# A hand-written order of 2,756 steps and its list of masked tiles, written anew

## The chip, the cores and the metric

One core of a Trainium2 chip runs the whole program. The metric is device time in microseconds (us) of one execution: median 465.35 us of three runs before the change (464.76 to 468.1). The engines are named as in the profile: PE is TensorE (PEld its weight loads), DVE VectorE, ACT ScalarE, POOL GpSimd, SP SyncE, which here only starts transfers.

## What is computed

Attention over 8 batches x 8 heads, 576 rows of 64, where only scores within tau = 0.02 of the row's maximum count; then a feed-forward layer with the largest of three products as its activation. Cut to the core:

```python
scores = (q @ k.transpose(0, 1, 3, 2)) / sqrt(64)
thresh = max(scores, axis=-1, keepdims=True) - tau
scores = where(scores >= thresh, scores, -1e9)
attn = exp(scores - max(scores)); attn = attn / (sum(attn) + 1e-9)
x = (attn @ v).transpose(0, 2, 1, 3).reshape(4608, 512)
h = maximum(maximum(x @ w1, x @ w2), x @ w3)     # 768 wide
out = h @ w_out                                   # 4608 x 512
```

## The kernel before

**Stages.** Four heads of a batch form a quad, so there are 16 quads, two to a batch. The 576 rows of a head are cut into chunks of 128; the rests of the heads share a chunk, so a quad has 9 chunks and the program 144. Each chunk has two tiles of scores (r = 0, 1), each 128 rows by 576 keys: 288 tiles. For every tile TensorE makes the scores in float32 (S). A quad's q and k must be turned first (T), by TensorE in float32, copied out by ScalarE (q) and VectorE (k); GpSimd copies a half-swapped q. Then, tile by tile, VectorE finds the row maximum (m), ScalarE makes exponents (e), and a last pass gives numerators and row sums. VectorE takes reciprocals (r), GpSimd scales to bf16 (p, once per tile), and SyncE starts one transposing DMA per chunk (t), which puts the chunk into ptq. When all nine chunks of a quad are there, TensorE makes the product with v (O, two per quad), which VectorE and ScalarE copy to xt. Per batch then follow 18 hidden pieces (F, and B for the second half of the same piece, evacuated by h and v) and the outputs (F and B, evacuated by u, stored by o). The last batch is split in two parts.

**The mask list.** A tile has two ways. If its digit in MASKED (line 24) is 1, VectorE copies the scores negated while it takes the maximum, ScalarE makes plain exponents, and VectorE sets those below exp(-tau) to zero and sums (k, a VectorE step). If it is 0, ScalarE makes two passes, the second with the sum (n). So a 1 moves work of some 0.7 us from ScalarE to VectorE.

**The order.** Every step of every engine stands in one string, ORDER (lines 38 to 70), read from left to right (lines 659 to 666). The class in lines 80 to 97 ties each instruction to the one before it on its engine, so each engine carries out its own letters in exactly the written order; between engines only data and buffers make them wait. S, T, O and F carry a digit, the PSUM bank pair (0 to 3) that the piece is written to. A piece can start only when the bank's last owner has been read. The other letters: a and c copy turned q and k out of PSUM, q is the swapped copy, l the next load of a quad (in turn: last columns of q and of k, 64 KB each, then the main parts of q and of k, 512 KB each, then v in two pieces of 256 KB and two of 32 KB), y a cast of v, g a load of 512 KB of weights and z its cast on GpSimd, x and w the copies of a product, h, v, u those of F pieces, o a store. The letters l, g, t and o all go to SyncE's one queue.

What each letter does is in issue (lines 596 to 657). The buffers: two of each loaded q, k, v and of ptq, four chunks of z, six of P.

Of the kernel before, what the change touches and what calls it, by code (L numbers as in the profile page):

```python
# [43 lines left out]
BmS3ezremF2pghkS1zetBmnF0vS3epgBnmF2pS1vetBmT0hS3rcpeF1S2rmpBmpteF0vpeBknS3ztF1nmS2vyeT3gzBmlO0hrlpalnpF1wle
T3ytBcnS0kS2nlmzO3nlrmeqlvelS2pS0rwxrmyF1npmS3gqBekqeF2vntpBmnS0pS1hmpgeS2mpeS3rmpeF0tmpeBrnS1pvS2tepmF0nzS3
metBrmpT2nS1vpaS3tnS0zmS2ermtpF1nkpnmS3eByrtmepkepF2lemlukS0utkBermnpoT1rekpoS0ecO3lupmtnpO1weoqurktpnS3T0xr
wS2mapoF1meT3qlS0cetBqmF3phS2kleqBmlF1nyF0lrnvBelpBrvS3yhpS2mnF1ptmS0epBmeF2ptvnF3BkeS1tvBnS0mhF2rmepS3rBepm
S1nytvF0peS3mpBnlmS2yetvT3eF1maS0lkBeqlS3mhlF2rmeplT1nlcpS0eBlrmpF1tnS3kpeBmnlO0qvernvtpT2S3wapS1nrmF2ptnS0m
# [5 lines left out]
rmBeptmeykS1yelS2mupS3lumO1temekT0oeF2ronwplakT3nT1qcS0nBpmnqtraS3peO1mqukuqonT0wS3rocpxS2lmeF0ptrF1mepBkpS3
thBremS0plvF2eptS3mS1ymeBlmF0pelS3veBmF2thS1keBknF0lmF3nlBveBlrknF2plS1rhvBnpmF3nS0pvtBepmF2rS1vtepBmpF0hT3k
tBerS2pavS1npF3mS0qmteBrmepO2vnpeS1twnS3mS0nF2meS1meBrmF0phS3knpBemO2eqvterkpT1xT0wS3caF2pnmT1qBtnrcF0pnvS3q
lBempF1lhS2rkyleBtmF0pvS3epBlrnmS1ypnvF2pterS3mpuS0meS2ptF1meymetS3knS0keBomnrmS2eplS3umpF0luroemptS2ekpT1em
T3oBakteqcT1nS2klaS3rmulpO1umoqeorkyeS0S2npmO3nprtwepmS1xpT0wtnmF2qS3ecpBlermF0qlhkS1pteBmnF2S3pvleBymlnF1vS
0eBtnmF2hS3keBlrmpF1nlvF0pnBlrpS2etvBynmS3S1hlrpmF2erpS0mteBpmeS3pvtnF0S1myeyF2pmeBktBeF3khT1vBaS2vnT0qS1rmp
O3meqcepS2wnF0tS1rnmpT3nmBpS2arvpS1temF3qeO0mpeketT2kxBnwS1clF0hrlmS2pnlBrkyeF3lmF1BrveqlBkpnF0lS2vhlBprmT3t  # L60
S1pvaS2pmeF0tS3mpeBkpteF1vnS2pmulS0moS1eF3metrmepS2knpS1S0nmBertmpekpS1nF2mertmpeS0kepS1mBuuqmtnS0keO3omeoku
O1urkoperowT2xpwT0cS3aqtS1nmF2qrF0myepBekS3yBhmF1pnS2vqteBmpnT0F3rcpelS2vBpnlS0mtphS1meS3mteF2knBmleS0lrnvpS
1ermF2plnS3pmteBpmF1eS0rveptBmnpF2kS3htBemF1nS0rvpleBmpF2nlrS3vpelT0mBtpaS1khS3qtmS0eqO2nmekerS3mpS1nmpO0ewt
ermpF2xwT3kpeF0cnBF1ntvT3BnkBarvS2phT3rrF0mqS1pceBmqtT3nS2pvS1ampS0eF3mpteF2mqeBkByeT1vhS0cT3pS2amF1qtnmF3qe
BkqBevS0nrF2vpT1rmupS3noS2cpnS0mpF1etmyeyrmpS2etkBepmnS3ktuS0urmF2peompnorS1kpeS3tmeS0BpmemteS1kuS0urS3kopnO
2ormepeO1pmnpweO0twrxmO2pxkS1eptS0xmnF3mS2teBkF0hmF1nBkS3ervF2peBmpBveS0ytF3hmS1F2emBkF0eBrvnpBrF1vphS3kpBtF
2mF0pveBytS3nyvO1kO2xrmF1xpBrkepS2BhmF3nptF0vepBF1ntvBS2hBmF3vS0eBrmpF1F2vpeBnS3thS0mBmF1eS3veBmnF0vO2urkepo
# [632 lines left out]
```

## Time and profile before

| what | value |
|---|---|
| median of three runs | 465.35 us |
| span of the profiled execution | 465.6 us |
| first piece of the order on TensorE, end of its last | 7.7 us, 460.8 us |
| POOL: P from z | 288 times 0.81 us, waits for DVE rs 58.5 us in all |
| ACT: e and n of tiles without mask | 0.74 and 0.68 us, 179 each |
| DVE: maximum of a tile | 0.75 us, 288 in all |
| transposing DMAs on SP | 144, 3.9 us from issue to landing (median) |
| main q and k loads, 512 KB each | 15 and 15, 4.4 and 5.5 us |
| bytes moved | 87.44 MB, 188 GB/s mean |

Times in the profile are those of one execution. An engine's idle time matters only where that engine, or one that it holds up, sets the end. The profile names for each idle stretch the instruction that ended it; a wait for a transfer is shown as DMA and the tile that it fills. The granted clock is the share of its full clock that TensorE was given.

### The profile page before, as it was taken

How to read it: one execution, taken by the hardware profiler on the slowest of the kernel's cores; microseconds unless marked ns; L12 is line 12 of the kernel's file. 1: busy time of each engine (PE TensorE's matmuls, PEld its weight loads, DVE VectorE, ACT ScalarE, POOL GpSimd, SP SyncE). 2: the span in 40 equal slices, each digit the busy share in tenths (PEclk: the TensorE clock that was granted, in tenths of full speed). 3: DMA queues.
4: the chain of work that ended last, by engine and by line, in shares of the span. 5: the costliest groups of instructions: out<-in, count | busy, mean ns of one | idle time of the engine just before them, and what ended most of it. 6: DMA issues, size and time to landing. Idle time of an engine off the chain costs nothing.

```text
span 465.6 us, 14101 instructions
## 1 busy us (share of the span) xinstructions
PE 437.9 (94%) x5188; PEld 314.1 (67%) x5188; DVE 403.9 (87%) x1115; ACT 394.0 (85%) x794; POOL 318.7 (68%) x416
## 2 busy tenths in 40 slices
PE   7778788999999999979999999999999999999995
...
PEclk8995899999999999979999999999999999999999
...
GB/s 256 242 210 232 199 222 246 166 237 275 216 232 183 212 161 230 221 215 135 207 214 229 130 189 212 212 196 220 160 190 224 153 84 223 105 102 66 173 32 103
DMA packets 212773, 87.44 MB, mean 188 GB/s; under 512 B 185824, under 2 KB 199648, under 8 KB 212704
## 3 DMA queue, kind: packets, MB, share of 16 engines
...
q14 instruction: 28, 0.23, 0.1%
...
## 4 chain that ended last, share of the span: by engine, by line
PE 70%; DVE 11%; ACT 11%; issue 5%; DMA 2%; POOL 0%; SPq 0%; ACTq 0%; DVEq 0%; POOLq 0%
PE sc L89 25%; PE ph L89 25%; ACT z L89 9%; PE po L89 8%; PE o L89 8%; DVE z L89 6%; PE tp L89 3%; DVE unused L89 2%; DMA ptq<-P 1%; DMA qm<-in_q_dram 1%; DVE kt L89 1%; DVE hT L89 1%; ACT xt L89 1%; ACT hm L89 1%; DVE hm L89 1%
## 5 line engine op out<-in xcount | busy, mean ns | idle before, releaser
L89 POOL TENSOR_SCALAR P<-z,rs 128x576 bf16<-128x576 f32 x288 | 229.5, 810 | 94.7 <-DVE rs L89 58.5
L89 PE MATMUL sc<-kt,qt 64*128 64x320 f32 (+2 forms) x640 | 192.7, 442 | 4.2 <-ACT z L89 2.2
L89 PE MATMUL sc<-kt,qs 64*128 64x256 f32 (+2 forms) x640 | 189.7, 431 | 6.2 <-ACT z L89 4.1
L89 PE MATMUL ph<-xt,w 64*128 64x288 bf16 (+2 forms) x2160 | 170.9, 283 | 1.2 <-DVE xt L89 0.3
L89 PEld LDWEIGHTS <-w 64*128 64x128 bf16 (+1 forms) x2160 | 125.0, 94 | 41.1 <-issue 12.6
L89 ACT ACTIVATE z<-sc,nm 128x576 f32<-128x576 f32 x179 | 129.9, 739 | 21.1 <-DVE unused L89 15.5
L89 DVE TENSOR_SCALAR_CACHE_REDUCE unused<-sc 128x576 bf16<-128x576 f32 x179 | 132.2, 749 | 8.2 <-PE sc L89 7.0
L89 ACT ACTIVATE z<-z 128x576 f32<-128x576 f32 x179 | 121.3, 680 | 0.3
L89 PEld LDWEIGHTS sc<-kt,qs 64*128 64x128 f32 (+1 forms) x640 | 93.2, 182 | 27.3 <-ACT z L89 7.4
L89 PEld LDWEIGHTS sc<-kt,qt 64*128 64x128 f32 (+1 forms) x640 | 93.1, 182 | 18.2 <-ACT z L89 6.7
L89 DVE SCALAR_TENSOR_TENSOR z<-z 128x576 f32<-128x576 f32 x109 | 93.3, 861 | 1.0 <-ACT z L89 0.9
L89 DVE TENSOR_SCALAR_CACHE_REDUCE z<-sc 128x576 f32<-128x576 f32 x109 | 81.1, 750 | 11.7 <-PE sc L89 9.9
L89 ACT ACTIVATE z<-z,nm 128x576 f32<-128x576 f32 x109 | 82.0, 771 | 9.8 <-DVE z L89 9.7
...
L89 PE MATMUL po<-wo,hT 64*128 64x512 bf16 (+1 forms) x480 | 54.2, 356 | 0.1
L89 ACT ACTIVATE hm<-ph 128x576 bf16<-128x576 f32 (+2 forms) x54 | 32.1, 595 | 16.2 <-PE ph L89 15.9
L89 DVE TENSOR_TENSOR hm<-ph,hm 128x576 bf16<-128x576 f32 (+2 forms) x54 | 36.9, 684 | 9.9 <-PE ph L89 9.1
L89 PE MATMUL o<-ptq,vb 128*64 128x64 bf16 (+2 forms) x544 | 40.6, 288 | 3.4 <-DMA ptq<-P 3.1
L89 PEld LDWEIGHTS <-hT 64*128 64x128 bf16 (+1 forms) x480 | 30.2, 97 | 17.6 <-issue 3.9
L89 DVE TENSOR_TENSOR hT<-ph,hm 128x576 bf16<-128x576 f32 (+2 forms) x54 | 37.0, 685 | 2.9 <-PE ph L89 1.4
L89 PEld LDWEIGHTS <-vb 128*64 128x64 bf16 x544 | 22.9, 113 | 20.9 <-issue 8.5
L89 ACT ACTIVATION_READ_ACCUMULATOR z<-z 128x1 f32 x179 | 35.4, 198 | 0.0
...
## 6 DMA issues: line engine op xcount, KB each, us to landing
...
ptq<-P SPq DMA_TRANSPOSE x144, 3.9
...
```

The lines of the kernel that those rows point to most:

```text
L89: ins = fn(*a, **kw)
```

## The change

Both strings are replaced. MASKED has 109 ones as before, at other places. ORDER has the same letters in the same numbers; their sequence and the bank digits differ. The first eight tokens now begin with a weight load and five loads of the second quad, where three of those loads came before the first S. No other line differs. Cut to the head, the stretch up to the first product of batch 3 (the O2 in the last of the three lines, on either side), and the end:

```diff
 MASKED = """
-101001010100010100100100100001010100000101000011000101010100000100100100
-000000111101010100001000101000001100100011011000110011000010100010010001
-000100110011000100111000010000101001001100011110000100100010010000111010
-100100101111001001000001000110110001100001010111001110011100100001101100
+101000100110000110011100001010010001100010001000101000010000100000100010
+000011110101100001001001001001000001011100101011000110001010010000010011
+001010011101100000101100100001001010000110011111000001000100000110000101
+001001001101100000110001000100101000001100010011100101110110000001111111
 """
...
 ORDER = """
-lllS0lmyS1eyS2lmlS3kelmnS0lmegS1repmgS2kyemnS3pT0meS1tmeymaS3S2knS0llremplekT3pnlrS1meqmnpmteprceT2qketS3pS0
-anT1rmS2lpnmS3qlempntrcS2pekT1eptS0mnqmelprkalS3petS1mnS2qrmnS0lperlmpetkpeT3mnlS1pmetS2mpnremptekyS0nS2qmlT
...
-lS0kuS3lakS1onF2rmpemlepS0rkepBtmnpmF3erqktepT1uBuconqroS0yuS2pumoS1pT3mteS0ympeO2koayntmO3ewqelrkS1qxlT2wS0
-rnmlpF3mlepcS1BleyF0tmphS2kpeBlmF3nF1lyveBtrknBpS0vhS2lpnrmF3S1pmetBpmeS0veS1tF2mnS3meBlmnF1F0lveBrelkpS2lBh
-mF3npF1vBetkS0nrrBvpF2mhpS3BeptmS1nyvT0T3nrmO2parcyetpS0ewqS3mnO1pmeptkeS2qT3xwS0mayF1meqF3kBeqBrnvT2pS0hclS
...
-O1S0xpS3mF1tmekS0eBmweF3rkpnkuS2pnBorrmupteF0pF1hF2nopvF0tuvpF1rhF2pvF0tvF1phF2vF0tvF1hF2uvF0ovF3hoF1vF2vF0h
-F3vF1vO2uoO0wF3xF1F2hF0vF1vF2hF0vF1vF2hF0vF1vF2hF0vF1vF2hF0vF1vF2hF0vBvF1uuooBF2uuouoo
+glllllS0lylS1mylyeS2zmlkS3lelmnlT0mS1aS2rmeqS0meqmeS3pnkT1pT0nrcaptemS0yeS1mgS2eympeS3mqtnT1S0mqnS2knrceprmS
+1epkepeS3mnyS0rkptemnS2pmnlzmS3erremtpT0empS1eklpaS2kgnS0ptnmeprrmlS1epS3mleS2pmlS0eplmetpmeS1knS3tkernkS2pt
...
+mparrcpS2uS1pumtS0empS3emqoS1eF2mqlemqleS3kplnS0mBlepmlekT1teO3kunktO0urcpnrrwlS2nplS1wxmpS3lmpS0eompS1eF2mt
+peF3meBkBetS0khF1nrmF2pnBvpBerrvS3phS0mtnpS1mF2peS3mtpeBmeF1yvF0etByknBvnS2tS3rhmpS1melpS0meF3lmF2elBkeBlvT1
+ntF0nvT3BacS2ohS1rrmlpnF3lmF0peoBkpeBovnT2oS1qavS3tnprO2rmpmleqS0wtnT3pS1mepO2mteqkeqF0nS1cxBywmpnS3rS2hytmS
...
+1tmBeBkO2vO0rvpF3kpF1uketeF3kekBwrrkpBukxpuF2F0hptF1vF2pvF0hF1tvF2rvpF0hF1vpF2vF0thF1uvF2uvF0hoF3vF1vF2hoF0v
+oO3oO1wovF2xF3uoF0F1hF2vF0vF1hF2vF0vF1hF2vF0vF1hF2vF0vF1hF2vF0vF1hF2vBvF0uuooBF1uuouoo
 """
```

More of the change, by code (lines that the diff above doesn't have):

```diff
@@ L44 @@
[L44 to L48, printed above, removed]
@@ L49 @@
-qBempF3hS1kqteO2meykT0rxrBwpceS2yvnS0ylmF1nlS3pmelF2pmtBeBkpeS0vhlS3nrtmF1pS2mepBrlmeF3ptS0vepS2mnBtmF1evnT2
-lS0kuS3lakS1onF2rmpemlepS0rkepBtmnpmF3erqktepT1uBuconqroS0yuS2pumoS1pT3mteS0ympeO2koayntmO3ewqelrkS1qxlT2wS0
-rnmlpF3mlepcS1BleyF0tmphS2kpeBlmF3nF1lyveBtrknBpS0vhS2lpnrmF3S1pmetBpmeS0veS1tF2mnS3meBlmnF1F0lveBrelkpS2lBh
-mF3npF1vBetkS0nrrBvpF2mhpS3BeptmS1nyvT0T3nrmO2parcyetpS0ewqS3mnO1pmeptkeS2qT3xwS0mayF1meqF3kBeqBrnvT2pS0hclS
-1ynmtF3nS2mpBelmpF1elS0vetBmnF3rS2veplBmnpF1S0rhkptBemF3nprS2vleBpmS0tnpvF1emS3tuS2rkepS1nrF0mopnmepS3tmeS2p
@@ L54 @@
[L54 to L67, printed above, removed]
-O1S0xpS3mF1tmekS0eBmweF3rkpnkuS2pnBorrmupteF0pF1hF2nopvF0tuvpF1rhF2pvF0tvF1phF2vF0tvF1hF2uvF0ovF3hoF1vF2vF0h
@@ L69 @@
-F3vF1vO2uoO0wF3xF1F2hF0vF1vF2hF0vF1vF2hF0vF1vF2hF0vF1vF2hF0vF1vF2hF0vBvF1uuooBF2uuouoo
+glllllS0lylS1mylyeS2zmlkS3lelmnlT0mS1aS2rmeqS0meqmeS3pnkT1pT0nrcaptemS0yeS1mgS2eympeS3mqtnT1S0mqnS2knrceprmS
+1epkepeS3mnyS0rkptemnS2pmnlzmS3erremtpT0empS1eklpaS2kgnS0ptnmeprrmlS1epS3mleS2pmlS0eplmetpmeS1knS3tkernkS2pt
+nmnprmtepmS1eqS0melpmT2ntrmT3pnrcpatekS3pekS2eqnrS1mtnqmS0pemepS3tmeqS2kepT1lnrcnprtmS0nT1pmS3epmgS2atpmeO1k
+yermeO0knptrerT3wpnT2wcS1aptmnS3pS2xmptS1emzS0emeS3zgmeS2lrmpnS0lmO1eplmeplknO3qlnrwleplwkS1xqgS2ertmF3npF0m
@@ new lines @@
+eT1pBrteBkyhS2cpnS3mpS1nvF2npmF0eqBmeqBrrvepS3tkhT2pS1nmS0lapmetS2pmeS3mzeF0mF1ezgBrnF2vpgnBktByeF0rvhpS3ntS
+2pmF1npmBeBqrveT3zncT0F2taqvS3nBpmnS0tprhS1rmpeS3mtpS2emeyS0mteF1zmeF3kBelqBnvgF2pngT0vBnqlrS1cphS3lrmnS0plm
+O2eplmeptS1ewpS3nmF0znmS2lBezkgO3etymyS1vegkF0ntF2wnrrmpBxBpveS3phS0mtnF1prmeBprS2evptS3nmF0pnS1mplBermS3ztn
+S2vnzS1meS0tmpeF3mperkS2petBmepmS0tkuF1ukelkT3elBkntrarmpS2uS3pmulS0eymtO1empnrO2kpewS3xpwS1elmpF2lmF0eyqBrl
+keT3ytBhcF1pnT2vT3qlaBclnS0qvlS2nqtF3mnyF1meS0pBemBthrrF2kpeS3vnBpmF0nS1pveBrprS3mhtS2pmeS0pmeS1tpmF2emF3peB
@@ new lines @@
+tkeT0BvaF1onvqT2T0tBcqaS3nkqS0lhrmS2nlpmF1elpF3meBlkBelF0vntS2rvnBpS1mhplS3melF0mS2teBrmepS1rkpO3emnqO2tnrvp
+nwyS0xlprwS3emoF2pmoT1eyBpctS3evyF0nS1mtnS2pmBeympF1hkS3eyF2rekT0ptBamBnpS0veF3qtvS1urmnpS2mF3epketT0nkT1Bnr
+mparrcpS2uS1pumtS0empS3emqoS1eF2mqlemqleS3kplnS0mBlepmlekT1teO3kunktO0urcpnrrwlS2nplS1wxmpS3lmpS0eompS1eF2mt
+peF3meBkBetS0khF1nrmF2pnBvpBerrvS3phS0mtnpS1mF2peS3mtpeBmeF1yvF0etByknBvnS2tS3rhmpS1melpS0meF3lmF2elBkeBlvT1
+ntF0nvT3BacS2ohS1rrmlpnF3lmF0peoBkpeBovnT2oS1qavS3tnprO2rmpmleqS0wtnT3pS1mepO2mteqkeqF0nS1cxBywmpnS3rS2hytmS
@@ new lines @@
+1emF0peF3mpeBrkBpetF2vnF1pBnvS0thkS3nmF2BmeBveF0rrvpT1uS3kapS0nmS2F1pmtepmeS3rktepS0mnS2pmlBelrmeplS3kupS0lu
+rmS2elpF1mnoqmeS0qreS2lmpS3elmBpelmptekO0nketO2ukurrnwpT3T1xwpcS0aF2ymyT3tpS1ceBqmS3thqF0meF2pknBtBnvF1nS3rt
+rvpeBmS0phS2lmepS1lmyS3etF0meyF2mpeBkBetF1knF3vnBBrvhpS0nvT1pF2nmF3takBeS0rvplBmS1phlrS2remplF3mpleF0klBpeS1
+lvnS2lpmnBtrO3mepvnptS2nwS1emF0mF3eBrkepS2hBrmS1nptvS0npT2meO3qmeycqlT0xT1wyS2lacF3ntmyT0yeF1kqBatrBrevqF0hk
+S2pnoS3mF1pmBteBpveS2qntS0vpnF3mprS1mlueS3pmoS0nqmtF2epmekT1oBerocpetrkS3npS1nmS0lpumS3uopmS1eT2mF0aokeorS3r
@@ new lines @@
+emplS2emtpS1emBpeklqtkO3uqunO0rtmpewpT2wxtS3cpeS0mnF2tF1meBknF3lkBhlBevF2nS0vnBmS1hrrS3pmeF0pmS2eBpmteF1pveF
+3kBlnS0vnlS2rrBnmlpS1hrlmpF0eF3mtpeBkpBevtS2nF1pvnT0pBtmaS3hS0metF1rmepT2BrcepS3nvptT0S2nmyS1amS3lepmS0leO2m
+lelmeO1rkpewnT3pwF0xcF2nykBnS1vnBrmS3phF0rrmepS2BynmqF1levF3qlBekpF0onvS2tBqmBhqrS1lepvT2S3lampF0lmS2peoBkpe
+tF1vnS3prmuS0ntqmS1eF2pmetpmeS3rkepS1tBmnpmelrS0keptS3muS1uymS0temT2yeF3pcntknT2BkelramtpS1nS2pmuS0leqrmO1tu
+qrkepO3nwepmS1xpwS2metF3pmS0eqBmeF1yhrkT2pBtecF3nS0vpnlS2rmpS1nlmBpnF0lveS2tmF3eBmeBkleF1klhF2lnrBvplS0nrrvp
```

8 lines of the change are left out of this document (5 added, 3 removed).

## The prediction

> **What bounds the kernel now.** I read the page's table of engines and its 40 slices first, then the busy time by stretch, then the waits and the chain where the stretches show a hole, and last SyncE's instructions ahead of that hole.
>
> ```profile
> PE 437.9 (94%) x5188; PEld 314.1 (67%) x5188; DVE 403.9 (87%) x1115; ACT 394.0 (85%) x794; POOL 318.7 (68%) x416
> PE   7778788999999999979999999999999999999995
> PEclk8995899999999999979999999999999999999999
> ```
>
> TensorE is the fullest engine, but it is thin at the start and has one notch in slice 18. The busy time by stretch (columns: stretch, length, then busy us with counts of PE, PEld, DVE, ACT, POOL, then granted clock, DMA share, GB/s) says how deep:
>
> ```profile
> 0.00:90.00 90.00, 72.04 (x666) 46.57 (x668) 75.40 (x219) 76.85 (x155) 69.71 (x91) 0.89 0.99 223
> 90.00:195.00 105.00, 104.07 (x1300) 74.85 (x1298) 98.81 (x272) 98.55 (x201) 84.22 (x110) 1.00 1.07 216
> 195.00:210.00 15.00, 11.79 (x126) 7.41 (x122) 8.60 (x23) 8.04 (x16) 8.04 (x13) 0.77 1.09 226
> 210.00:450.00 240.00, 239.28 (x3019) 179.12 (x3016) 217.15 (x595) 206.47 (x417) 156.69 (x204) 1.00 0.84 167
> 450.00:465.60 15.60, 10.73 (x91) 6.10 (x89) 3.94 (x8) 4.04 (x9) 0.00 (x0) 0.99 0.21 77
> ```
>
> From 90 to 195 and from 210 to 450 TensorE stands still for 0.9 and 0.7 us: there only its own work counts, and no order changes that. Before 90 us it has too little to do, since batch 0 must pass ScalarE and VectorE before any F piece can start. At 195 to 210 all engines lose time together. The waits there (engine and tile, releaser: us, times, longest), the chain (start, us, what) and SyncE's instructions (start, us, what):
>
> ```profile
> ACT z L89 <- DVE unused L89: 5.7, 1, 5.7
> PE o L89 <- DMA ptq<-P: 3.1, 1, 3.1
> ```
> ```profile
> 198.15 5.35 DMA ptq<-P
> ```
> ```profile
> 192.16 0.57 SPq L89 DMA_DIRECT2D km<-in_k_dram  x1
> 192.78 0.47 SPq L89 DMA_DIRECT2D qm<-in_q_dram  x1
> 193.34 1.24 SPq L89 DMA_TRANSPOSE ptq<-P  x1
> 194.64 0.81 SPq L89 DMA_DIRECT2D km<-in_k_dram  x1
> 195.54 5.95 SPq L89 DMA_TRANSPOSE ptq<-P  x2
> ```
>
> The first product of batch 3 (O2 in line 52) waits for the transposes of its last chunk. That chunk was ready at 189.5, but SyncE came to it only at 198.2. The landings are 197.4 (qm), 198.7 (transpose), 201.5 (km), 202.5 and 203.5 (transposes): in the order of issue, 2.8 us for a 512 KB load behind the landing before it and 1.0 for a transpose. Two such loads stood in front. Matching each written t with its transpose in the trace, SyncE runs 2 us behind its place at 151 us and 8 us behind at 190; every other engine stays within about 1 us of its place.
>
> **The change part by part.** I take the profiled execution: span 465.6. The median of the three times is 465.35, so 0.3 comes off at the end.
>
> *The mask list.* 109 ones before and after, of 288; 128 places differ. Work per engine is unchanged, so nothing by itself; where the ones fall goes into the start below.
>
> *TensorE's pieces.* The same pieces. Median distance of starts in the trace: S 0.54 (0.69 for chunk 4), F and B halves 0.49, O 1.36, outputs 1.30 a half, T 0.30 to 0.36. Their sum is 420 in both orders. Actual pace against these prices loses 29 us up to 90 us, 6.5 in the notch, 2.5 from 90 to 195 us, and wins 5 in the last 45 us, where F pieces of whole rows are quicker. The last 20 tokens differ in bank numbers alone, so the end is worth 0.
>
> *The start.* Along each order I add ScalarE's work (0.64 to 0.68 per e, 0.675 per n, 0.46 to 0.55 for the rest, the back-to-back spacings in the trace) and subtract TensorE's. The largest surplus is what TensorE must stand still for. Old: 66.8 - 46.3 = 20.4, at the sixth F. New: 80.7 - 61.4 = 19.4, in batch 1. That is **-1.0**. The rest of the 29 is waiting around it, which I carry over.
>
> *A weight load in front.* The new order begins with g, so a 512 KB stage transfer goes ahead of the second quad's q and k. Such a transfer took 1.3 and 2.2 us from the landing before it (14.75, 16.02, 18.23). The q load landed at 11.4 and now lands at 12.7 to 13.6. The first T now stands after 4 S pieces instead of 8; the fourth S ended at about 11.6, so TensorE, with S1 and S2 queued behind the T, waits 1.1 to 2.0 us. ScalarE's next work is that T's own evacuation; it has some 0.6 us of n left, so it loses 0.5 to 2.0. I take **+1.3**, the middle. The early z (1.15 us on GpSimd) is hidden because the q copies behind it wait for the same T anyway; uncovered it would cost 1.1.
>
> *The second quad.* The last k evacuation for quad 2 is now written directly before the S piece that reads it (5.5 us of TensorE work apart before). Between 0 and one evacuation, 0.75 (the row of kt); I take 0, because ScalarE has written work waiting there, and keep 0.7 for the range.
>
> *Products.* 15 pairs of O stand back to back, 8 before. Banks and evacuations are the same in number. In the saturated stretches this costs 0; in batch 0 it can delay fresh scores by at most 2 x 1.36 = 2.7, covered by exponents already pending, so 0, with 2.7 kept.
>
> *SyncE's order, the main term.* For every first product of a quad I add what is written on the transfer queue in the 14 us of TensorE work up to the last transpose (1.0 per transpose, 2.8 per 512 KB load, 0.8 per 256 KB, 0.3 to 0.5 for small ones). After the first batch the old order has more than 14 us in seven quads; ahead of the O that stalled it has 15.6, the most of all. The new order has 12.9 at most, and 12.5 ahead of that O: both of its big loads come before six transposes in a row instead of among them. From TensorE's place 60 to 180, SyncE's own issue time (1.37 per transpose, 0.64 per other) falls from 97 to 90, the rest moved later, so its lag has no cause to reach 8 us. Price of the stall: TensorE's wait of 3.1 and the clock at 0.77 over 15 us, 0.23 x 15 = 3.45; together 6.6. ScalarE's pause alone gives 5.7, the piece prices 6.5. I take **-6.5**. What is late next is TensorE itself, saturated on both sides of the notch.
>
> Sum: 465.6 - 1.0 + 1.3 - 6.5 - 0.3 = **459.1**.
>
> **A rule against it.** The Trainium skill (DMA: Bandwidth & Descriptors, sections Queues, rings and completion order and Two DMAs through the same engine are not ordered) says that completion is not first in, first out: a later transfer may finish before an earlier one, and nothing orders transfers across the 16 engines. By that rule, moving loads past transposes would not set the landing, and the 6.5 would stay. The five landings above, all in the order of issue, speak against it here; what it would make of the time is the first rival.
>
> **The rivals.**
>
> *The stall comes from volume, not order.* The transfers are the same 87 MB, and the DMA share is 1.07 from 90 to 195. Then a notch of the same price returns: 459.1 + 6.5 = 465.6. For it: that share. Against: transposes elsewhere landed 4 us after issue (median 3.9), with the same share. Chance 0.13.
>
> *Slower: SyncE's lag stays, on thinner margins.* In the old order the time from the last t's place to its landing, in TensorE work, was 9.5 (batch 2, second quad), 13.1 (batch 3, first), 6.6 and 5.6 (batch 5), 4.9 (the last quad). The new order leaves 10.0 at batch 3 but only 8.9, 5.7, 4.9 and 3.8 at the others. With the old needs the shortfalls are 0.6, 3.1, 0.9, 0.7 and 1.1 = 6.4 of waiting, plus 3.4 for one clock drop: 459.1 + 9.8 = 468.9, or 472.3 with two drops. It decides as soon as the needs do not fall below those margins. For it: batch 5's second quad still has 13.4 us of SyncE work in 14. Against: the queue ahead is lighter nearly everywhere. Chance 0.14. The Trainium skill (TensorE: Matmul & The Clock Gate, Part 1) lets the clock drop only after an idle window of about 3.4 us, which favours the lower figure; the wait of 3.1 in this trace did drop it.
>
> *A better start.* Of ScalarE's waits from 9.5 to 90 us (7.4 in sum) much is for maxima. The new order writes exponents further behind their maxima (mean VectorE work between them 0.98 against 0.88). If that saves 3, the time is 456. Chance 0.14.
>
> The forecast has 0.55, and 0.04 is left for something unseen that costs several us.
>
> **How the numbers follow.** About 1% (4.7 us) is what this kernel's measurement can tell from no change: 460.7 and 470.0 are the borders. The forecast's own range is 456.5 to 462, from the ends kept above, and I put 0.41 of its 0.55 under 460.7. Faster: 0.41 + 0.14 = 0.55. Same: 0.14 + 0.13 + 0.06 of the slower rival = 0.33. Slower: 0.08 + 0.04 = 0.12. The range 454 to 468 takes in the better start with 2 us to spare, the notch that stays with 2.4, and leaves out most of the slower rival.
>
> **What would show it.** Right: no wait of TensorE on ptq over 1 us, the clock at 1.00 from 90 to 450, a time for 90 to 450 that holds the same work in about 6.5 us less, and transposes landing some 4 us after issue throughout. The weight load: a wait of 1 to 2 us of a tp piece on qm near 12 us. Wrong: a wait on ptq in batches 2 to 6, a clock under 1.00 after 90 us, or a loss before 90 us that grows beyond 31 us.

## The result, and the profile after

| | before | after |
|---|---|---|
| median, four runs each | 465.64 us (464.76 to 468.1) | 451.9 us (451.11 to 452.89) |
| ratio of the times, 95% interval | | 0.9673 [0.9627, 0.9719] |
| span of the profiled execution | 465.6 us | 449.3 us |

The forecast was 459.1 with a range from 454: the change gave twice what was expected of it, and the time lies below the range. The ratio is the recorded estimate; the quotient of the two medians is 0.9705. The spans differ by 16.3, the medians by 13.7. An execution takes 1.8 us more than its span (451.11 for 449.3, and about as much in the other runs), so that the profiled execution before was some 2 us slower than the median of these four. It is not an odd one: in the later batches, of 13 to 25 executions each, the median of the kernel before was 466.5 to 468.2. What follows splits the 16.3.

From the page of the changed kernel, its table of engines and two of its 40-slice rows:

```profile
PE 425.6 (95%) x5188; PEld 314.8 (70%) x5188; DVE 402.0 (89%) x1115; ACT 392.3 (87%) x794; POOL 314.8 (70%) x416
PE   6766889999999999999999999999999999999995
PEclk8989999999999999999999999999999999999999
```

TensorE has no notch any more: slice 18 is as full as its neighbours and keeps its clock. The busy time by stretch (columns as in the prediction):

```profile
0.00:90.00 90.00, 71.91 (x736) 47.62 (x738) 78.95 (x229) 80.52 (x163) 74.02 (x98) 0.96 1.01 226
90.00:195.00 105.00, 104.38 (x1336) 79.03 (x1331) 100.80 (x278) 99.59 (x204) 79.77 (x106) 1.00 1.12 216
195.00:210.00 15.00, 15.00 (x204) 11.25 (x202) 14.13 (x40) 13.85 (x29) 11.34 (x16) 1.00 0.92 213
210.00:434.00 224.00, 223.90 (x2839) 170.98 (x2836) 204.15 (x563) 194.58 (x394) 149.71 (x199) 1.00 0.89 179
434.00:449.30 15.30, 10.42 (x89) 5.89 (x86) 3.94 (x8) 3.76 (x8) 0.00 (x0) 0.97 0.21 78
```

The third row shows the step that was foreseen: TensorE 15.00 of 15 us busy at clock 1.00, where it had 11.79 at 0.77. The first two show what was not. In the first 90 us TensorE finished 736 matmuls in place of 666, at the same busy time, and ScalarE and VectorE were busy 3.7 and 3.6 us longer. From 90 to 195 us TensorE's busy time is the same within 0.3 us (104.38 and 104.07), yet it holds 36 matmuls more. A count mixes small matmuls with large ones, but the table below, which does not, agrees: a full engine did more work in the same time.

SyncE's instructions ahead of the first product of batch 3, which starts at 195.3 (start, us, what):

```profile
175.93 10.89 SPq L89 DMA_TRANSPOSE ptq<-P  x6
186.87 1.39 SPq L89 DMA_DIRECT2D vm<-in_v_dram  x2
188.31 1.27 SPq L89 DMA_DIRECT2D vr<-in_v_dram  x2
189.69 1.30 SPq L89 DMA_TRANSPOSE ptq<-P  x1
```

The six transposes stand in a row with no 512 KB load of q or k between them, and the last of the quad had landed 6.6 us before this product started. Before, it had landed after the product's turn.

**Where the time went, at equal work.** The written orders tell which piece each record belongs to. Both traces can then be read at the same amount of TensorE work done (each piece at its median distance to the next, 421 us in all), instead of at the same time. The lead of the new kernel, in us:

| work done | 30 | 55 | 110 | 160 | 170 | 230 | 330 | end |
|---|---|---|---|---|---|---|---|---|
| time before | 61.2 | 91.8 | 148.7 | 198.9 | 215.3 | 275.1 | 375.5 | 460.8 |
| lead | +1.7 | +5.1 | +6.1 | +7.1 | +13.3 | +13.4 | +15.1 | +16.3 |

So 5.1 come in the start, 6.2 in the notch (work 160 to 170), and 5.0 a little at a time in the long stretches where both kernels look saturated. All experiments below are read by this curve too; theirs is always the lead over the same profile of before. A curve is one execution. Up to 30 us of work, executions of the same steps differ by up to 3 us (reached at 59.0 to 61.2 us with the old start, at 58.8 to 61.6 with the new), so the 1.7 won there is not above that scatter. Behind it the same steps repeat far more closely: the work from 280 to 330 took 50.2 to 50.5 us in the eight kernels of this document that keep the old steps there, and 49.4 to 49.5 in the eight that have the new ones.

### The profile page after: what moved, and what is told of

Its sections match the earlier page's. It is cut to its first block, busy times and chain, and to the rows that moved or that the text cites. A ratio compares the mean times of both kernels' runs of the same rounds, so it can differ in the third digit from the quotient of the medians.

```text
span 449.3 us, 14063 instructions
## 1 busy us (share of the span) xinstructions
PE 425.6 (95%) x5188; PEld 314.8 (70%) x5188; DVE 402.0 (89%) x1115; ACT 392.3 (87%) x794; POOL 314.8 (70%) x416
## 4 chain that ended last, share of the span: by engine, by line
PE 75%; DVE 6%; POOL 5%; DMA 5%; ACT 3%; issue 3%; SPq 1%; ACTq 0%; POOLq 0%; DVEq 0%
PE ph L89 30%; PE sc L89 26%; PE po L89 8%; PE o L89 8%; POOL P L89 3%; PE tp L89 3%; DVE z L89 3%; DVE unused L89 2%; ACT z L89 2%; DMA ptq<-P 1%; SPq L89 1%; DMA qm<-in_q_dram 1%; DMA km<-in_k_dram 1%; POOL qs L89 1%; ACT ob L89 1%
## 5 line engine op out<-in xcount | busy, mean ns | idle before, releaser
L89 PE MATMUL sc<-kt,qs 64*128 64x256 f32 (+2 forms) x640 | 180.2, 421 | 9.2 <-ACT qt L89 3.2
L89 PE MATMUL sc<-kt,qt 64*128 64x320 f32 (+2 forms) x640 | 181.2, 432 | 4.0 <-DVE kt L89 1.2
L89 PE MATMUL ph<-xt,w 64*128 64x288 bf16 (+2 forms) x2160 | 165.0, 283 | 0.3 <-DVE hm L89 0.2
L89 PEld LDWEIGHTS <-w 64*128 64x128 bf16 (+1 forms) x2160 | 127.1, 94 | 29.4 <-issue 6.7
L89 ACT ACTIVATE z<-sc,nm 128x576 f32<-128x576 f32 x179 | 128.8, 742 | 11.6 <-DVE unused L89 9.7
L89 DVE TENSOR_SCALAR_CACHE_REDUCE unused<-sc 128x576 bf16<-128x576 f32 x179 | 130.3, 751 | 4.0 <-PE sc L89 3.4
L89 PEld LDWEIGHTS sc<-kt,qs 64*128 64x128 f32 (+1 forms) x640 | 91.5, 178 | 33.3 <-ACT z L89 7.8
L89 PEld LDWEIGHTS sc<-kt,qt 64*128 64x128 f32 (+1 forms) x640 | 91.6, 177 | 21.0 <-ACT z L89 6.5
L89 DVE SCALAR_TENSOR_TENSOR z<-z 128x576 f32<-128x576 f32 x109 | 89.9, 839 | 0.3 <-ACT z L89 0.2
L89 POOL COPY qs<-qt 64x640 f32<-64x640 f32 (+1 forms) x62 | 45.4, 733 | 14.7 <-ACT qt L89 11.6
L89 DVE TENSOR_TENSOR hm<-ph,hm 128x576 bf16<-128x576 f32 (+2 forms) x54 | 37.1, 687 | 12.1 <-PE ph L89 11.6
L89 PE MATMUL o<-ptq,vb 128*64 128x64 bf16 (+2 forms) x544 | 38.9, 281 | 0.2
```

The source lines that it names most:

```text
L89: ins = fn(*a, **kw)
```

## The experiments

But for the last, every kernel has the same pieces; its order is edited, and bank digits follow where they must. Medians shift between batches, so ratios, each against before in its own batch, are what is compared. "Work" is TensorE's, as above. Diffs show one line that differs, where more of an order is another one.

### The notch: order of the transfers or their volume

**old_loads_late.** The old order, three loads (k8, q, k of the tenth quad) behind the transpose that the stalled product needs:

```diff
-rnmlpF3mlepcS1BleyF0tmphS2kpeBlmF3nF1lyveBtrknBpS0vhS2lpnrmF3S1pmetBpmeS0veS1tF2mnS3meBlmnF1F0lveBrelkpS2lBh
+rnmlpF3mlepcS1BleyF0tmphS2kpeBmF3nF1yveBtrknBpS0vhS2pnrmF3S1pmetBpmeS0veS1tlllF2mnS3meBlmnF1F0lveBrelkpS2lBh
```

> The old order with three steps of SyncE moved: the 64 KB k load and the two 512 KB loads of the tenth quad go from among the last transposes ahead of the first product of batch 3 to just behind the last of them; nothing else. Theory (the queue's order made the stall): the wait of O on ptq near 200 us and the clock drop behind it go, 6.5 us less, some 459 us. Rival (volume made it, the transfers are the same): the wait stays or comes back near 200 us, 464 to 467 us.

461.87, ratio 0.9893 [0.986, 0.9926]: 5.0 us less on 465.6, and a lead that grows from 0.7 to 5.3 between 160 and 170 us of work. TensorE's waits from 180 to 230 us (engine, tile, releaser: us, times, longest) and the stretch around them:

```profile
PE o L89 <- DMA ptq<-P: 1.0, 1, 1.0
```
```profile
195.00:210.00 15.00, 13.92 (x188) 10.00 (x186) 12.15 (x33) 11.77 (x26) 11.56 (x17) 1.00 1.17 220
```

The wait of 3.1 is 1.0, the clock keeps 1.00, with the same bytes at a DMA share of 1.17. Order sets this wait.

**new_loads_between.** The opposite on the new order: six loads (q, k, v of one quad) ahead of a transpose near 290 us. Here the T pieces that turn this quad's q stand ahead of the moved loads and read the tile before it is filled.

```diff
-3kBlnS0vnlS2rrBnmlpS1hrlmpF0eF3mtpeBkpBevtS2nF1pvnT0pBtmaS3hS0metF1rmepT2BrcepS3nvptT0S2nmyS1amS3lepmS0leO2m
+BnS0vnS2rrBnmpS1hrmpF0eF3mtpeBkpBevtS2nF1pvnT0pBlllllltmaS3hS0metF1rmepT2BrcepS3nvptT0S2nmyS1amS3lepmS0leO2m
```

> The new order with six loads of quad 12 (q, k, v) moved down to just ahead of the last transpose that the first product of batch 5 needs. Theory (queue order): that transpose lands some 7 us later, against a margin of 2.1 us in the new order, so O waits 4 to 5 us on ptq near 298 us and the clock drops once, 456 to 460 us. Rival (volume): the same transfers in the same 30 us, no wait over 1 us, 451 to 453 us.

456.81, ratio 0.9781 [0.9723, 0.9839]. The loss is there, but it sat in a wait of T for a load (3.1 us on km), not in one of O for a transpose. This does not decide between the two, so the next one moves loads that nothing needs so early:

**new_loads_between2.** Nine loads of two later quads gathered ahead of the 81st transpose:

```diff
-rvpeBmS0phS2lmepS1lmyS3etF0meyF2mpeBkBetF1knF3vnBBrvhpS0nvT1pF2nmF3takBeS0rvplBmS1phlrS2remplF3mpleF0klBpeS1
+rvpeBmS0phS2mepS1myS3etF0meyF2mpeBkBetF1knF3vnBBrvhpS0nvT1pF2nmF3llllllllltakBeS0rvpBmS1phrS2rempF3mpeF0kBpe
```

> The new order with nine loads of quads 10 and 11 (three of 512 KB, two of 256 KB, four small) gathered just ahead of the last transpose that the first product of batch 4 needs; in the new order two of them (512 and 256 KB) stood some 7 us earlier and seven behind it. All data arrive before they are used. Theory (queue order): the transpose lands some 8 us later against a margin of 2.1 us, so O waits about 6 us on ptq near 245 us and the clock drops, 457 to 461 us. Rival (volume, the transfers of the stretch are the same): no such wait, 451 to 453 us.

457.8, ratio 0.9814 [0.9759, 0.9869], some 6.6 us more than the new kernel's 0.9673 and 6.1 more than new_g_later (below) in the same batch; by its curve the lead falls from 11.8 at 180 us of work to 7.1 at 230, by 4.7. Its waits from 225 to 260 us and that stretch:

```profile
PE o L89 <- DMA ptq<-P: 2.9, 1, 2.9
```
```profile
240.00:255.00 15.00, 12.14 (x136) 8.57 (x132) 10.29 (x30) 9.50 (x21) 6.71 (x9) 0.89 1.01 241
```

A notch was made where there was none, by order alone. The first rival, volume, falls: some 5 us can be taken out and put in elsewhere with the same 87 MB.

### The start and the rest apart

Ten kernels follow one order up to a certain work done and the other from there on (newheadN is new until N us of work and old behind, oldheadN the reverse). The diffs show the line at the seam.

**newhead55**, **oldhead55**. Against the new order and against the old:

```diff
-2pmF1npmBeBqrveT3zncT0F2taqvS3nBpmnS0tprhS1rmpeS3mtpS2emeyS0mteF1zmeF3kBelqBnvgF2pngT0vBnqlrS1cphS3lrmnS0plm
+2pmF1npmBeBqrveT3zncT0F2taqvS3nBpmnS0tprhS1rmpetegmS3etmS3eF1S2mpBmpteF0vpeBkkS3ztF1nmS2vegzBmlO0hrlplnpF1wl
```
```diff
-BmS3ezremF2pghkS1zetBmnF0vS3epgBnmF2pS1vetBmT0hS3rcpeF1S2rmpBmpteF0vpeBknS3ztF1nmS2vyeT3gzBmlO0hrlpalnpF1wle
+BmS3ezremF2pghkS1zetBmnF0vS3epgBnmF2pS1vetBmyT3cT0aqrhrppS2yS0meF1zmeF3nBelqBnvF2pngT0vBkqlrS1cphS3lrmnS0plm
```

> The new order (and its mask places) until TensorE has 55 us of its own work written, some 87 us into the run; from there every step not yet written follows in the old order with the old mask places. Theory (the start's 5 us are made by the order before that place): 5 us ahead of the old order at 90 us and all the way, notch at O of batch 3 as before, 459 to 462 us. Rival (the start's gain is a loan that the old order takes back, ScalarE and VectorE being no further on with their work there): 464 to 466 us.

> The old order until TensorE has 55 us of its own work written, then the rest in the new order with its mask places. Theory (the start, the notch and small waits later are separate parts that add): the start's 5 us are lost, the notch and the 4 to 5 us of small waits behind the start are won, 455 to 458 us. Rival (the later small gains hang on the new start): only the notch is won, 459 to 460 us.

newhead55: 466.94, ratio 0.9989 [0.9955, 1.0023]; its lead was 4.4 at 55, 2.1 at 70, and 2.0 from there to 160; the wait at the product, 3.5, was back. oldhead55: 455.89, ratio 0.9754 [0.9678, 0.9831]; lead 0.4 at 55, 1.6 at 160, 7.8 at 170, 11.0 at the end. The remainder of the new order wins its 11 without its start. The start wins nothing clear of the interval once the old remainder follows; 2.3 are lost behind the seam.

**oldhead20**, **oldhead30**, **newhead30**, where in the start. Against the old order twice, and against the new:

```diff
-1nzrcaemT1pS3ekpteS0mnS2yrmqelcplnS3rplnmS1tpemS2epmS0tepmS1nrS3mptekpT0erlekO2qtamnpS0melpmleS1kteT3rmnpS0l
+1nzrcaemT1pS3ekpteS0mnS2yrmqelcplnS3rplnmS1tpemzgpenS2ekrS0mtnmS3pemepS1tmeqS2kepnrnprtmS0nT1pmS3epmgS2atpme
```
```diff
-nqmleprwnS1qeS2pmtnS0mpeO1czntrmnpS3wekT0permT2aptkeS0pxS3rcnS1gpmtnS2rpmepmetS0mqnO3qmegprnS2wynS0mS1etprmO
+nqmleprwnS1qeS2pmtnS0mpeO1czntrmnpS3wekT0permggyaxptS1zS0meS3zgmeS2rmpkS0mO1epmepnnO3nrwepwkS1xgS2ertmF3npF0
```
```diff
-yermeO0knptrerT3wpnT2wcS1aptmnS3pS2xmptS1emzS0emeS3zgmeS2lrmpnS0lmO1eplmeplknO3qlnrwleplwkS1xqgS2ertmF3npF0m
+yermeO0knptrerT3wpnT2wcS1aptmnS3pS2xmptlllllllqlqeemT1neS0pS3rckS1pmtnS2rpmepmetS0mqnO3qmeprnS2wnS0mS1etprmO
```

> The old order and mask until 30 us of TensorE work are done (some 60 us), the new ones from there on. If the start's gain is made in the first 30 us of work, it is gone here and the ratio is that of the kernel that was old until 55 us of work, 0.975 (some 455.5). If it is made between 30 and 55 us of work, most of it is kept: ratio 0.967 to 0.970 (452 to 453.5). A new wait at the seam would add 1 to 2 us to either.

> The new order and mask until 30 us of TensorE work, the old ones from there on. Start's gain made in the first 30 us and kept: ratio 0.993 to 0.995. Made later, or a loan that is paid back at the seam, as in the kernel that was new until 55 us of work: ratio 0.998 to 1.002; the wait at the third product of the fourth quad near 200 us is there in both cases, 2 to 4 us.

> The old order and mask until 20 us of TensorE work (some 45 us), the new ones from there on. If the start's gain is made behind this point, where ScalarE's idle time of 20 to 92 us lies in the old heads: ratio 0.966 to 0.970 (as the new kernel's 0.967), and 86 to 88 us at 55 us of TensorE work. If it is made ahead of it, or if the seam costs what it did at 30 us of work: 0.975 to 0.980 and 91 us or more.

oldhead20: 451.93, ratio 0.969 [0.9634, 0.9746], as fast as the new kernel; lead -0.1 at 30, 3.3 at 55, 15.2 at the end. So the start's gain is made behind 20 us of work (some 45 us on the clock). newhead30: 469.74, ratio 1.0044 [1.0009, 1.0079], lead -0.1 at 30 and 0.3 at 55: nothing is won before. oldhead30 (459.49, ratio 0.9799 [0.9774, 0.9825]) says little of this, since its seam brought a wait of its own. Its waits from 55 to 82 us:

```profile
ACT z L89 <- POOL P L89: 5.6, 1, 5.6
POOL w L89 <- DMA stage<-in_moe_w_dram: 5.2, 2, 3.6
```

GpSimd stood at a cast of weights whose transfer came late in this mixed order, P behind it was late, and ScalarE had no free z.

What the fullest engine of the start did, over all traces, up to 55 us of work (ScalarE's idle time from 20 us on):

| start | kernels | time at 55 us of work | ScalarE idle |
|---|---|---|---|
| old | before, old_loads_late, oldhead55, old_pairs, oldhead170 | 91.8, 89.3, 91.4, 91.3, 92.0 | 6.2, 3.1, 5.4, 5.2, 5.5 |
| new | after, newhead55, new_loads_between, new_loads_between2, new_split, new_g_later, newhead110, newhead110_late, newhead170, newhead192 | 86.7, 87.3, 87.5, 88.2, 87.1, 87.7, 86.0, 86.7, 88.8, 87.2 | 1.1, 1.6, 2.1, 1.0, 1.4, 1.9, 1.1, 1.0, 2.1, 1.6 |

The means are 91.2 and 87.3 us, with 5.1 and 1.5 of idle time: of the 3.8 us between them, ScalarE's idle time covers 3.6.

The same traces place the gain more narrowly. From 30 to 55 us of work the six kernels with the old steps there took 30.2 to 31.8 us, the eleven with the new ones (oldhead20 is one; oldhead30, with its seam at 30, is left out) 27.2 to 27.3; ScalarE stood idle there for 2.4 to 3.9 us and for 0.1 to 0.3. Between the profiles of before and after this is 3.4 of the 5.1 us. It also answers a rival, that the granted clock made the start's gain. In the first 60 us TensorE lost 10.05 us to clock stretches of about 0.5 before, and as much in newhead192 (clock 0.89, 0.83, 0.73 and 0.88 in four windows of 15 us), which has the new start and still reached 55 us of work at 87.2 in place of 91.8. From 60 to 90 us both were at 1.00.

ScalarE's waits from 12 to 92 us, before:

```profile
ACT z L89 <- DVE unused L89: 2.3, 5, 0.7
ACT z L89 <- DVE rs L89: 1.8, 2, 1.4
ACT qt L89 <- PE tp L89: 1.5, 1, 1.5
ACT z L89 <- DVE z L89: 0.5, 1, 0.5
```

and after:

```profile
ACT qt L89 <- PE tp L89: 1.0, 1, 1.0
ACT z L89 <- DVE z L89: 0.4, 1, 0.4
ACT z L89 <- DVE unused L89: 0.4, 1, 0.4
```

4.6 us of waiting for VectorE became 0.8. The largest of them, 1.4, stands in the timeline of before:

```profile
78.20 1.03 POOL L89 CAST w<-stage 128x1024 bf16<-128x1024 f32 x1
78.35 2.20 DVE L89 SCALAR_TENSOR_TENSOR z<-z 128x576 f32<-128x576 f32 x1
79.21 0.74 POOL L89 TENSOR_SCALAR P<-z,rs 128x576 bf16<-128x576 f32 x1
81.29 0.48 PE L89 MATMUL sc<-kt,qs 64*128 64x256 f32 x1 [1.30 <-DVE hT L89]
82.14 0.76 DVE L89 TENSOR_SCALAR_CACHE_REDUCE unused<-sc 128x576 bf16<-128x576 f32 x1 [0.23 <-PE sc L89]
83.00 0.74 ACT L89 ACTIVATE z<-sc,nm 128x576 f32<-128x576 f32 x1 [1.44 <-DVE rs L89]
```

A masked numerator on VectorE, median 0.76 us, took 2.20 while GpSimd ran a cast and a P beside it. VectorE's hT behind it was late by as much, TensorE waited 1.30 for that step to free a bank, and the score that it then made (81.29) was the one whose maximum (82.14) ScalarE needed. The Trainium skill (SBUF — State Buffer, section SBUF: two separate sides) has VectorE with two SBUF inputs and GpSimd lock one another out of a shared port for a whole instruction; that fits this row. It does not explain the gain by its amount: what the numerators took above their median is 11.9 us before and 9.5 after over all 109, but 3.5 and 3.7 over those ahead of 55 us of work. At most the place of these delays differs. What is shown is that the new steps between 30 and 55 us of work keep ScalarE from waiting; which of them does it, by the order or by the mask list, no run separates.

**newhead110**, **newhead110_late**, **newhead170**, **newhead192**, **oldhead170**: does an old remainder keep a lead? The second has the three loads of old_loads_late moved as well. Against the new order, newhead110, the new order twice, and the old:

```diff
-tkeT0BvaF1onvqT2T0tBcqaS3nkqS0lhrmS2nlpmF1elpF3meBlkBelF0vntS2rvnBpS1mhplS3melF0mS2teBrmepS1rkpO3emnqO2tnrvp
+tkeT0BvaF1onvqT2T0tBcqaS3nkqS0lhrmS2nlpmF1elpF3meBlkBelF0vntS2rvnooomplpS1elrmptS3pemnlO2erktpS3wpS1nrmptnS2
```
```diff
-rnmlpF3mlepcS1BleyF0tmphS2kpeBlmF3nF1lyveBtrknBpS0vhS2lpnrmF3S1pmetBpmeS0veS1tF2mnS3meBlmnF1F0lveBrelkpS2lBh
+rnmlpF3mlepcS1BleyF0tmphS2kpeBmF3nF1yveBtrknBpS0vhS2pnrmF3S1pmetBpmeS0veS1tlllF2mnS3meBlmnF1F0lveBrelkpS2lBh
```
```diff
-ntF0nvT3BacS2ohS1rrmlpnF3lmF0peoBkpeBovnT2oS1qavS3tnprO2rmpmleqS0wtnT3pS1mepO2mteqkeqF0nS1cxBywmpnS3rS2hytmS
+ntF0nvT3BacS2ohS1rrmlpnF3lmF0peoBkpeBovnT2oS1qavS3tnprO2rmpmleqS0wtnT3pS1mepO2mteqkeqF0nS1cxBywmpnS3rS2hytml
```
```diff
-rmS2elpF1mnoqmeS0qreS2lmpS3elmBpelmptekO0nketO2ukurrnwpT3T1xwpcS0aF2ymyT3tpS1ceBqmS3thqF0meF2pknBtBnvF1nS3rt
+rmS2elpF1mnoqmeS0qreS2lmpS3elmBpelmptekO0nketO2ukurrnwpyyyllyylltoolT3T1cktaqqonT0wS3ocpxS2lmF0ptrF1mepBnpS3
```
```diff
-1ynmtF3nS2mpBelmpF1elS0vetBmnF3rS2veplBmnpF1S0rhkptBemF3nprS2vleBpmS0tnpvF1emS3tuS2rkepS1nrF0mopnmepS3tmeS2p
+1ynmtF3nS2mpS1emeF0mpeBrnBpetF2vF1pBnvS0thkS3nmF2BmeBveF0rrvpT1uS3kapS0nmS2F1pmtepmeS3rktepS0mnS2pmBermepS3k
```

> The new order and mask until 110 us of TensorE work (some 143 us), the old ones from there on, the third product's wait near 200 us among them. If the lead of the start (about 5 us at that point) is real, the rest runs as the old one did and ends 3.5 to 5.5 us ahead: ratio 0.988 to 0.993. If it is a loan that ScalarE and VectorE must pay back wherever the new order ends: ratio 0.997 to 1.001, with the curve of gains falling by 3 to 5 us within 20 us behind the seam.

> The kernel that was new until 110 us of TensorE work and old from there on, with three loads of the tenth quad (k8, q, k) put behind the transpose that the third product of the fourth quad needs. If the lead that was left ahead of this product (2.5 us) had been lost to the landing of that transpose alone, taking the wait away gives both the 5 us that the same move gave in the old order and these 2.5: ratio 0.983 to 0.986. If the old remainder takes the lead back in any case: 0.988 to 0.991, as the move alone.

> The new order and mask until 170 us of TensorE work (behind the place of the third product of the fourth quad, some 202 us), the old ones from there on. If what the new order gains ahead of this place (start about 5, up to the products 2, the wait 6.5) is kept by an old remainder: 13 us less what a seam costs, ratio 0.972 to 0.977. If an old remainder takes back every lead but that of the wait: 6 to 8 us, ratio 0.983 to 0.987.

> The new order and mask until 192 us of TensorE work, the old ones from there on: as the kernel cut at 170, at a place where no load that is due soon has still to be issued (there GpSimd waited 8.5 us for a load of V that the new order issues later, and the 10.9 us won until then were gone). What is late here are five casts of V on GpSimd, some 4 us of its time. If the lead of some 11 to 13 us is kept by an old remainder that has its loads: ratio 0.972 to 0.980. If an old remainder takes the lead back in any case: 0.985 or more.

> The old order and mask until 170 us of TensorE work, the new ones from there on. If the new remainder is faster by itself by the 3 us that the profiles show behind this place: ratio 0.992 to 0.995. If that part of the gain hangs on a lead made ahead of it: 0.998 to 1.002.

| kernel | ratio [95%] | lead at 55 | 110 | 125 | 160 | 170 | 180 | 230 | end |
|---|---|---|---|---|---|---|---|---|---|
| newhead110 | 1.0002 [0.9979, 1.0026] | 5.7 | 5.2 | 2.5 | 2.5 | 0.5 | 0.4 | 0.1 | -1.3 |
| newhead110_late | 0.9901 [0.9867, 0.9936] | 5.0 | 5.7 | 3.0 | 3.0 | 8.8 | 8.8 | 8.5 | 7.2 |
| newhead170 | 1.0031 [0.9988, 1.0073] | 3.0 | 4.5 | 4.7 | 5.5 | 10.9 | -0.7 | -0.7 | -4.5 |
| newhead192 | 0.9953 [0.9921, 0.9986] | 4.6 | 3.9 | 4.1 | 4.9 | 11.1 | 10.9 | 4.0 | 3.3 |
| oldhead170 | 0.9923 [0.9891, 0.9955] | -0.3 | -0.6 | -0.6 | -0.7 | 1.0 | 0.3 | 0.5 | 3.5 |

By their times newhead110, newhead170 and newhead192 all fell on the side of an old remainder that takes the lead back. The curves show how: the lead is lost in steps, and the larger ones behind the seam have a wait for a transfer. In newhead110, 2.7 go at the seam, where TensorE waits 2.2 us for ScalarE and GpSimd and no transfer shows, and 2.0 in the notch. Its wait there:

```profile
PE o L89 <- DMA ptq<-P: 5.5, 1, 5.5
```

The transpose landed at 203.4, as before it did at 203.5, though the work ahead of it ran 2.5 us early: what TensorE had won, it waited. In newhead55, 2.0 us early there, it landed at 201.9, and the wait was 3.5. newhead170 lost 11.6 at once. Its waits from 198 to 225 us:

```profile
ACT z L89 <- POOL P L89: 9.7, 1, 9.7
POOL vb L89 <- DMA vm<-in_v_dram: 8.5, 1, 8.5
PE sc L89 <- ACT z L89: 8.4, 1, 8.4
```

The new order issues its loads of V later in the work than the old one. A remainder that counts on the earlier place finds them missing, and the wait goes from GpSimd's cast through P and z to TensorE. newhead192, cut where those loads had been issued, met another wait of a product for a transpose, 3.9 us near 246. Between such waits a lead shrinks by no more than 1.6: newhead192 goes from 4.0 at 230 to 3.3 at the end, newhead110_late from 5.7 at 110, past its 2.7 at the seam, to 8.8 behind the notch and 7.2 at the end. By its curve newhead110_late kept what newhead110 lost in the notch; by its times (0.9901) it is no better than old_loads_late (0.9893). Part of this lies in which execution was profiled: that of newhead110_late took 460.24 us with a median of 462.41, that of old_loads_late 464.48, the longest of its ten, with a median of 461.87. By the times the lead of 2.5 was not kept; the rest stays open. newhead170's curve is of the longest of its ten executions too (471.97, median 467.73), so its -4.5 at the end is worse than is usual for it. oldhead170 did as the own-gain theory said: the new remainder alone is worth 0.9923, 3.6 us.

### The long stretches

In eight traces the curve rises where the new steps run and is flat or falls where the old ones do. From 170 us of work to the end: after +3.0, oldhead20 +3.0, oldhead55 +3.2, new_g_later +3.2, oldhead170 +2.5; newhead30, newhead55 and newhead110 -2.4, -1.1 and -1.8. The gain belongs to the steps there, and not to the lead that they start with.

What in them does it? The pieces are the same, but their neighbours are not. Medians of the distance to the next start, both traces together: a product 1.26 us ahead of another product, 1.36 ahead of a score; the first half-tile score of a chunk 4 0.48 ahead of the second, 0.70 ahead of an F piece (the second is 0.65 to 0.69 ahead of either). The two stand side by side in 5 of the 16 quads before and in 15 after. The old order changes its kind of piece on TensorE 426 times, the new one 336 times. Priced by neighbour, the pieces behind 55 us of work come to 360.5 and 357.3: 3.2 of the 5.0, and from 170 to 330, 159.0 and 157.5 where 160.2 and 158.3 were measured. The prices are medians of these same traces, and other ways to group neighbours give 2.7 to 5.2. Without prices, behind 170 us of work the chunk-4 scores took 11.1 us before and 9.4 after, 1.7 of the 3.0 won there. TensorE's busy time hides this, but the idle time of its weight loads (releaser "issue" where nothing that the profile shows ended it) does not. Before, from 105 to 460 us:

```profile
PEld L89 <- issue: 21.0, 63, 0.7
```

and after, from 105 to 445 us:

```profile
PEld L89 <- issue: 11.8, 37, 0.5
```

The Trainium skill (Perfetto Trace Analysis, section Identifying the Most-Contended Engine) warns that matmul busy time is a bad measure because matmuls are pipelined, and names the busy share of weight loads as a good one; here the first went from 94 to 95% and the second from 67 to 70%, with 3.5% off the span.

**new_split** parts 12 pairs of products and 6 of chunk-4 scores in the new order; **old_pairs** puts 10 pairs side by side in the old one. The first changed line of each:

```diff
-S2vnzS1meS0tmpeF3mperkS2petBmepmS0tkuF1ukelkT3elBkntrarmpS2uS3pmulS0eymtO1empnrO2kpewS3xpwS1elmpF2lmF0eyqBrl
+S2vnzS1meF3tmpeS0mperkS2petBmepmS0tkuF1ukelkT3elBkntrarmpS2uS3pmulS0eymtO1empnrS2kpewO3xpwS1elmpF3lmF0eyqBrl
```
```diff
-BmS3ezremF2pghkS1zetBmnF0vS3epgBnmF2pS1vetBmT0hS3rcpeF1S2rmpBmpteF0vpeBknS3ztF1nmS2vyeT3gzBmlO0hrlpalnpF1wle
+BmS3ezremF2pghkS1zetBmnF0vS3S2epgBnmF1pvetBmT0hS3rcpeF1S2rmpBmpteF0vpeBknS3ztF1nmS2vyeT3gzBmlO0hrlpalnpF1wle
```

> The new order with 18 neighbours on TensorE parted behind its first 55 us of work: 12 pairs of O and 6 pairs of chunk-4 S pieces get the piece that followed them in between; banks of 23 pieces change with that. Theory (a piece costs less behind one of its own kind: O before O 1.26 against 1.36 us, chunk-4 S before S 0.48 against 0.69, S before O 0.63 against 0.54): 2.6 us more by these spacings, 453 to 456 us. Rival (the later small gains come from looser spacing of the other engines' steps, not from neighbours): within 1 us of the new order.

> The old order with 10 of its O pairs and chunk-4 S pairs put side by side on TensorE (7 of S, 3 of O; the others have no bank for it); banks of 20 pieces change. Theory (neighbours): 1.8 us less by the same spacings, 463 to 465 us where the old order has 465 to 467. Rival: the moved pieces make new waits on other engines that take it back, 465 to 468 us.

new_split: 466.92, ratio 0.9998 [0.9971, 1.0025], 15 us more than the new kernel for 18 moves by one place. old_pairs: 473.0, ratio 1.0147 [1.0104, 1.019]. Both lost far more than neighbours can account for. Piece by piece, though, the prices came as expected. In old_pairs the three moved products went from 1.36 to 1.43 us down to 1.26 to 1.30, and the seven half-tile scores from 0.70 or more to 0.48 to 0.69, three of them to 0.48; in new_split the nine parted products of whole batches went from 1.26 to 1.31 up to 1.36 to 1.81, and the scores from 0.48 to 0.52 up to 0.70 to 1.17. new_split's waits of TensorE from 95 to 460 us begin with:

```profile
PE o L89 <- ACT z L89: 0.8, 2, 0.6
PE ph L89 <- DVE hT L89: 0.7, 2, 0.5
PE ph L89 <- DVE z L89: 0.7, 2, 0.4
PE ph L89 <- DVE xt L89: 0.6, 3, 0.2
```

Small waits of many kinds, where the new kernel has two of 0.2. All of TensorE's waits in that list come to 4.8 us, a third of the 15; where the rest went stays open. The 18 moves, with 23 banks changed and no reader on the other engines moved along, came to some 0.85 us each. So the price by neighbour is seen at the pieces that were moved and fits the sums, but no run turned it into time: how much of the 5.0 it made is argued.

### Two single terms

**new_g_later.** The new order, with its first weight load behind the second quad's loads, and its cast later:

```diff
-glllllS0lylS1mylyeS2zmlkS3lelmnlT0mS1aS2rmeqS0meqmeS3pnkT1pT0nrcaptemS0yeS1mgS2eympeS3mqtnT1S0mqnS2knrceprmS
+lllllS0lylS1mylgyeS2mlkS3lelmnlT0mS1aS2rmeqS0meqmeS3pnkT1pzT0nrcaptemS0yeS1mgS2eympeS3mqtnT1S0mqnS2knrceprmS
```

> The new order with its first step, the weight load g, moved behind the eight loads of the second quad, and its cast z moved behind the second p. Theory of the prediction (ScalarE binds the start, the wait of the first T on qm of 1.3 us near 13 us is lost for good): that wait goes and the time falls by 1.3 us, 450 to 451 us. Rival (the wait is taken up by slack later in the start, or the later weights hold up the first F): no change, 451 to 453 us.

451.68, ratio 0.9689 [0.9651, 0.9727]. T's wait of 1.3 for q is gone, and the time is not less.

**old_filler.** The old order, with an extra transpose on TensorE behind every score piece of the first 26 chunks, to keep its clock up:

```diff
+        if number[L["b"] * (H // 4) + L["qd"], idx] < 26:
+            tensor.transpose(ps[:, 0:128], identf, identf)
```

> The old order, with one more small TensorE transpose of an identity after each score piece of the first 26 chunks, into columns that nobody reads (extra work, same output). Clock theory: the half-clock stretches of the first 60 us (10.0 us lost by the granted clocks of the before profile, 15-us windows) come from a TensorE that is idle too much, and they cost the start; then the windows from 15 to 60 us show a clock near 1.00 and the time falls by 2 to 3 us, ratio about 0.994. Rival, ScalarE and VectorE set the start whatever the clock: the clock may change, the time does not fall; the extra transposes cost 0 to 3 us, ratio 1.000 to 1.007.

Four executions took 485.91, 497.39, 497.81 and 502.26 us against 468.16 before in its batch: even the shortest is 17.7 us longer. In the profiled one, of 497.39, the clock did what was wanted, but the price was misjudged. The page's row of the clock, and the row of the added pieces in the groups of TensorE (busy, mean ns):

```profile
PEclk9999999999999999999999999999999999999999
```
```profile
L89 PE MATMUL sc<-identf 128*128 128x128 f32 x52 | 22.4, 430 | 0.0
```

The groups of TensorE before had it: the 12 warm-up transposes, of the same form, took 425 ns each, so that 52 of them are 22 us and not the 0 to 3 of the expectation. The shortest execution had a mean clock of 0.973, the profiled one 0.999, so the higher clock came with no shorter time. What the half-clock stretches of the start cost is not settled by this run. They differ between runs of one and the same start (1.65 us lost in the first 60 us in newhead110, 6.75 in new_loads_between, 10.05 in newhead192), while these reach 55 us of work at 86.0, 87.5 and 87.2.

**Not tried.** Exchanging the mask list alone: order and list are one plan, since a mask decides which engine reads a bank, and neither order has free banks at the right places with the other list.

## Why the prediction was wrong, point by point

- *SyncE's order, the main term*, -6.5: right. 6.2 at equal work in the new kernel, 6.2 in oldhead55, and some 5 when taken out or put in by itself.
- *The start*, -1.0: this step failed, at "The rest of the 29 is waiting around it, which I carry over." The lead at 55 us of work is 5.1 in the profile and 3.8 in the means over all starts, most of it between 30 and 55 us of work, where new steps take some 3.5 us less than old ones in every trace. The count took ScalarE's work and TensorE's, and left VectorE out, which held ScalarE up for 4.6 us before and 0.8 after. My third rival, "A better start", had this mechanism and a size of 3, and its 456 came nearest. I gave it 0.14.
- *TensorE's pieces*, 420 in both orders: failed too, at the sentence that "there only its own work counts, and no order changes that." The time of its own work depends on the neighbour. The long stretches gave 5.0 in place of 0, of which the neighbour prices explain about 3.2; the rest stays open. The 5 us seen as won in the last 45 us were read wrongly too, with no effect on the sum: F pieces of whole rows take 0.44 and 0.55 us for the two parts, no less than two halves of 0.49, while the half products of the split batch take 0.6 to 0.8 us in place of 1.36.
- *A weight load in front*, +1.3: the wait came as foreseen (1.3, at 13.2 us), the price did not. new_g_later took the wait away and won nothing: ScalarE is full from 15 to 45 us all the same (29.92 of 30 us with the wait, 29.65 without).
- *The mask list*, *The second quad*, *Products*: 0 each; no wait of their kind shows. In the start the mask list can't be told from the order.
- The offset of -0.3 stood for the difference of a span to a median. The runs show some 1.8 us between span and time, and a profiled execution that was about 2 us slower than the median of its batch; the two happened to cancel, which is luck.
- *The rivals*: volume fell with old_loads_late and new_loads_between2. "SyncE's lag stays, on thinner margins" did not come: no product waited in the new kernel, though some margins are thin, 0.1 and 0.2 us at the second quads of batches 0 and 1, 1.9 at the least from batch 2 to 6, and 0.8 and 0.2 in batch 7. The rule of the Trainium skill that was weighed there (DMA: Bandwidth & Descriptors, Two DMAs through the same engine are not ordered) would have let the moved loads make no difference; on this one queue they made some 5 us, both when moved out and when moved in.

With the terms as measured the sum is 465.6 - 5.1 - 6.2 - 5.0 = 449.3, the new span. It has to come out, since the three are a division of the 16.3; that the parts belong to the steps, and not to chance, rests on the mixed orders.
